# Seven products instead of eight in the first layer of three experts, running sums in PSUM, and all sums on VectorE

## The chip, the core and the metric

The kernel runs on one core of a Trainium2 chip. The core has five engines that work through queues of their own, each in the order in which the program was laid out: TensorE (matmuls; PE in the profile, its weight loads PEld), VectorE (DVE), ScalarE (ACT), GpSimd (POOL) and SyncE (SP, which here starts DMA transfers). They wait for one another by semaphores. The metric is the time of one execution on the device in microseconds.

## The reference

Two blocks follow one another. The first is a recurrent attention (RWKV-5) over 4 batches, 8 heads, 768 steps and a head size of 48; its output becomes `x`, 3072 rows of 384. The second gives each row to one of eight experts, 384 rows to each, and sends it through that expert's two layers:

```python
def _moe_ref(x, w_gate, w1, w2):
    N, D = x.shape                       # 3072, 384
    E = w_gate.shape[1]                  # 8
    cap = N // E                         # 384
    order = np.argsort(-(x @ w_gate).flatten())
    ...                                  # the best pairs (row, expert) first, until an expert is full
    for e in range(E):
        mask = assigned == e
        h = np.maximum(x[mask] @ w1[e], 0.0)    # 384x384 times 384x1024
        out[mask] = h @ w2[e]                   # 384x1024 times 1024x384
```

All inputs and the output are fp32.

## The kernel before

**Attention (0 to about 150 us)** runs in `Mild` over units of 128 steps of one batch. The change does not touch it.

**The search.** `Assignment` finds which expert fills next and with which rows, without leaving the chip. One round of `likely_steps` compares every row's value with 16 candidates (`ind`, L932), counts with matmuls (`counts`, L944 and L955, the second of which reads `wide`) and narrows the interval three times, mostly on VectorE; then come `acc`, a matmul for the places (`st_ps`, L1075), `row`, `oh` and `vals`, and two small matmuls (`some_ps` L1408, `list_ps` L1426) that give the list of rows `tok`. So VectorE and TensorE hand this chain to and fro while TensorE works on an expert.

**The experts.** `Experts.run` goes through the experts in the order in which they fill, n = 1 to 8; n = 8 is the rest of an expert that was begun during the attention and has 128 rows. While expert n is worked on, `later` takes the search on, and `fetch` gathers the rows of the next expert (`xg`, on POOL's queue) and loads its weights (`load_weights`, on SP's queue, w2 first, then w1). Weights and rows lie in two sets of buffers, `turns[n % 2]`, so expert n+2 is loaded when expert n releases its own.

For each expert of 384 rows:

- `turn` transposes the gathered rows to `xT`: three blocks of 128 inner elements, 384 rows wide.
- `hidden` is the first layer: for each of eight tiles of 128 of the 1024 hidden columns, three matmuls (one for each inner block) of a 128x128 weight tile with 384 columns of `xT`, summed in one bank of PSUM; ScalarE writes the ReLU to `hid`.
- The second layer of experts 1 to 5 is `seven` for the first 256 rows. `hid` and w2 are cut in halves both ways, and the four products of halves are had from seven, with sums of blocks before and after (Winograd's form of Strassen's scheme). `sums_of` makes the sums of blocks on VectorE: T1 to T4 of w2 (768 elements a lane), S1 to S4 of `hid` (512). `products` runs the matmuls in groups, one bank a group; ScalarE copies each group to `res`, and VectorE adds there (`SEVEN_OUT`, eight sums of 192 elements). The last 128 rows go through `result`, eight matmuls of 384 columns.
- The second layer of experts 6 and 7 (`many`) is `fifteen`, by fifteen products for all 384 rows, with eleven sums of `hid` (two of them, `EARLY_SUMS`, made at half of the first layer), ten of w2 and 24 of the results.

Order: the framework's scheduler lays out each engine's queue from the program order and its own estimates; nothing in this part is placed by hand, apart from `issue_after` for the first expert. An instruction that waits holds up everything behind it on its engine.

Names in what follows: `hid<-h_ps` is the ReLU (L1543), `h_ps` the first layer (L1541), `p_ps` the products (L1616), `o_ps` the last 128 rows (L1643), `S`, `T`, `H` and `W` the sums of blocks (L1593).

Of the kernel before, what the change touches and what calls it, by code (L numbers as in the profile page):

```python
# [10 lines left out]
F32 = mybir.dt.float32  # L11
# [4 lines left out]
AF = mybir.ActivationFunctionType  # L16
# [1432 lines left out]
def rwkv5_eagle_then_base_layer_balanced(  # L1449
# [12 lines left out]
    nc = tc.nc  # L1462
# [21 lines left out]
    class Experts:  # L1484
# [7 lines left out]
        def open_rest(self, ctx, **how):  # L1492
            pool = lambda name, bufs, **kw: ctx.enter_context(tc.tile_pool(name=name, bufs=bufs, **kw))
            self.h, self.o, self.sums = pool("f_h", 2, **how), pool("f_o", 2, **how), pool("f_sums", 1, **how)
            self.ps_t, self.ps_h, self.ps_o = (pool(f"f_ps_{x}", 2, space=PSUM, **how) for x in "tho")

        def load_weights(self, n, fmax):
# [34 lines left out]
        def turn(self, ahead):  # L1532
            *_, xT = self.turned(ahead, lambda c: self.ps_t.tile([128, KD, 128], F32, name="xT_ps"))
            return xT

        def hidden(self, w1, xT, m, half, progress):
            hid = self.h.tile([128, KF, CAP], F32, name="hid")
            for j in range(KF):
                h_ps = self.ps_h.tile([128, CAP], F32, name="h_ps")
                for f in range(KD):  # L1540
                    nc.tensor.matmul(h_ps[:, 0:m], w1[:, f, ts(j, 128)], xT[:, f, 0:m],  # L1541
                                     start=(f == 0), stop=(f == KD - 1))
                nc.scalar.activation(hid[:, j, 0:m], h_ps[:, 0:m], AF.Relu)  # L1543
                if j == KF // 2 - 1:
                    half(hid)
                progress((j + 1) / KF)
            return hid
# [1 line left out]
        BLOCKS = dict(h0=(0, 0), h1=(0, 1), h2=(1, 0), h3=(1, 1), h4=(2, 0), h5=(2, 1))  # L1549
        SEVEN_EARLY = (("S3", "h0", SUB, "h2"),)  # L1550
        SEVEN_LATE = (("S1", "h2", ADD, "h3"), ("S2", "S1", SUB, "h0"), ("S4", "h1", SUB, "S2"))
        SEVEN = ((("p1", "h0", "w0"), ("p2", "h1", "w2")), (("p7", "S3", "T3"), ("p5", "S1", "T1")),
                 (("p6", "S2", "T2"), ("p3", "S4", "w3")), (("p4", "h3", "T4"),))
        SEVEN_OUT = ((("o0", "p1", ADD, "p2"),), (), (("u2", "p1", ADD, "p6"), ("u3", "u2", ADD, "p7"),
                     ("u4", "u2", ADD, "p5"), ("o1", "u4", ADD, "p3"), ("o3", "u3", ADD, "p5")),
                     (("o2", "u3", SUB, "p4"),))
        EARLY_SUMS = (("H1", "h0", ADD, "h2"), ("H11", "h0", SUB, "h4"))
        HID_SUMS = (("H8", "h1", ADD, "h3"), ("H7", "h1", SUB, "h0"), ("H9", "h1", SUB, "H11"),
                    ("H3", "h5", SUB, "H9"), ("H0", "h1", ADD, "h2"), ("H6", "h3", ADD, "h5"),
                    ("H5", "H11", ADD, "H6"), ("H2", "h2", SUB, "H6"), ("H12", "H2", ADD, "h4"))  # L1560
        W2_SUMS = (("W11", "w0", "w3"), ("W7", "w0", "w1"), ("W9", "W7", "w3"), ("W13", "W9", "w4"),
                   ("W0", "W13", "w5"), ("W14", "W0", "w2"), ("W12", "w0", "w2"), ("W5", "W12", "w3"),
                   ("W6", "W5", "w5"), ("W2", "W6", "w4"))
        PRODUCTS = ((("p4", "h4", "w1"), ("p1", "H1", "w2"), ("p11", "H11", "W11"), ("p10", "h5", "w4")),
                    (("p8", "H8", "w5"), ("p13", "h1", "W13"), ("p7", "H7", "W7"), ("p9", "H9", "W9")),
                    (("p3", "H3", "w3"), ("p0", "H0", "W0"), ("p14", "h2", "W14"), ("p5", "H5", "W5")),
                    (("p12", "H12", "W12"), ("p6", "H6", "W6"), ("p2", "H2", "W2")))
        OUT_SUMS = ((),
                    (("x", "p9", SUB, "p4"), ("u", "x", SUB, "p7"), ("o0", "u", ADD, "p11"), ("t", "p13", SUB, "p11"),
                     ("o1", "t", SUB, "x"), ("o7", "p10", ADD, "p4")),  # L1570
                    (("o6", "u", ADD, "p3"), ("y", "p13", ADD, "p14"), ("z", "y", SUB, "p0"), ("o2", "p1", SUB, "z"),
                     ("o5", "z", ADD, "p8"), ("d", "p11", SUB, "p5"), ("v", "p1", ADD, "d")),
                    (("g", "p12", SUB, "o6"), ("o3", "g", SUB, "v"), ("q", "p6", SUB, "o5"), ("o8", "q", ADD, "v"),
                     ("a", "p14", SUB, "p2"), ("b", "p10", ADD, "p6"), ("o4", "a", SUB, "b")))
# [7 lines left out]
        def seven_w2(self, w2):  # L1582
            H, D = KF // 2, DX // 2
            at = {f"w{2 * j + k}": w2[:, ts(j, H), ts(k, D)] for j in range(2) for k in range(2)}
            self.sums_of(at, (("T3", "w3", SUB, "w1"), ("T1", "w1", SUB, "w0"), ("T2", "w3", SUB, "T1"),
                              ("T4", "T2", SUB, "w2")), D)
            return at

        def sums_of(self, at, which, n=128):
# [7 lines left out]
        def fifteen(self, left, right, tok, rows, at_product):  # L1597
            self.products(self.PRODUCTS, self.OUT_SUMS, left, right, tok, rows, at_product, KD, NC)

        def seven(self, left, right, tok, rows, at_product):  # L1600
            self.products(self.SEVEN, self.SEVEN_OUT, left, right, tok, rows, at_product, 2, 2)

        def products(self, products, out_sums, left, right, tok, rows, at_product, nk, ni):
            D = DX // nk
# [35 lines left out]
        def result(self, c, hid, w2, tok, to):  # L1640
# [8 lines left out]
            nc.scalar.copy(o_sb, o_ps)  # L1649
            self.scatter(o_sb, tok[:, c:c + 1], to)  # L1650

        def run(self, ahead, later, rows, pulls={}, xT=None):
            xT, lead = xT or self.turn(ahead), True
            while ahead:
                n, _, tok, w1, w2 = ahead
                nb = tok.shape[1]
                whole = nb == NC
                many = whole and n in (E - 2, E - 1)
                ahead = next((a for a in later if a), None)
                late, lead = lead and not many, False  # L1660
                right = (self.fifteen_w2 if many else self.seven_w2)(w2) if whole and not late else None
                left = {}
                some = pulls.get(n, 2)
                due = [1.55, 1.75] if some == 2 else [0.75 + 1.15 * i / (some - 1) for i in range(some)]

                def half(hid):
                    nonlocal right
                    for name, (i, j) in self.BLOCKS.items():
                        left[name] = hid[:, ts(j, KF // 2), ts(i, 128)]
                    last = self.sums_of(left, self.EARLY_SUMS if many else self.SEVEN_EARLY)  # L1670
                    if late:
                        with tc.issue_after(last.ins):
                            right = self.seven_w2(w2)

                def progress(t):
                    nonlocal xT
                    while due and t > due[0]:
                        due.pop(0)
                        next(later, None)
                        if many and not due and ahead:  # L1680
                            xT = self.turn(ahead)

                def at_product(part):
                    progress(1 + part)

                hid = self.hidden(w1, xT, nb * 128, half if whole else lambda hid: None, progress)
                if whole:
                    self.sums_of(left, self.HID_SUMS if many else self.SEVEN_LATE)
                    (self.fifteen if many else self.seven)(left, right, tok, rows, at_product)
                    if many:  # L1690
                        continue
                for c in range(NC - 1 if whole else 0, nb):
                    if c == nb - 1 and ahead:
                        xT = self.turn(ahead)
                    self.result(c, hid, w2, tok, next(rows))

        def early(self, ps, pool, w1, w2, xg, tok, rows, have):
# [182 lines left out]
```

## Time and profile before

| | |
|---|---|
| Median of 3 runs | 398.09 us (398.03 to 398.3) |
| The profiled execution | 397.39 us |
| its span, from the first to the last instruction | 395.7 us |
| granted TensorE clock, mean | 0.997 |
| first layer, TensorE: 384 instructions | 120.7 us busy |
| products of the second layers, 128x192 `p_ps<-w,hid`: 80 instructions | 14.7 us busy, 333 ns one |
| the last 128 rows of five experts and the eighth: 96 instructions | 33.1 us busy |
| ScalarE's ReLU, 128x384: 56 instructions | 27.5 us busy, 491 ns one |
| weight transfers: 18 of 1.5 MB | 10.2 us median from issue to landing |

A page lists for each engine how long it was busy, for forty equal slices of the span in tenths how busy each engine was, then the costliest groups of instructions by line. A group's row has the shape, the count, the busy time, the mean length of one, the engine's idle time just before, and what ended that. A length of a matmul runs to its modelled end, beyond the start of the next one, so the spacing of starts says more than the length. The stages of the experts are found in TensorE's timeline: expert 2 runs from 188.0 to 220.5 us, expert 3 to 253.1, expert 4 to 285.7, expert 5 to 317.7, expert 6 to 348.3, expert 7 to 378.1 and the rest to the end.

### The profile page before, as it was taken

The page shows a single profiled execution, that of the slowest core. Times are in us where ns is not written, and L with a number is a line of the kernel's source. Part 1 is how long each engine was busy: PE and PEld are TensorE (multiplying, and loading weights), DVE is VectorE, ACT ScalarE, POOL GpSimd, SP SyncE. Part 2 cuts the span into 40 slices and gives each one's busy share as a digit, 9 for nine tenths or more (in the row PEclk, how much of TensorE's full clock was granted, in tenths as well). Part 3 has the DMA queues.
Part 4 walks back from the last instruction along what each step waited for, and adds up shares of the span by engine and source line. Part 5 has one row for each costly group of instructions (what it writes and reads, how often), then busy time and mean ns, then how long its engine had stood idle before and what let it go on. Part 6 is the DMA issues. An engine that isn't in the chain of part 4 may idle for free. (4 is left out here: it accounts for less than half of the span.)

```text
span 395.7 us, 8692 instructions
## 1 busy us (share of the span) xinstructions
PE 381.1 (96%) x3243; PEld 289.3 (73%) x3243; DVE 266.9 (67%) x934; ACT 162.0 (41%) x429; POOL 138.4 (35%) x173
## 2 busy tenths in 40 slices
PE   7899999999999999999999999999999999999993
PEld 5678888888877765587578569558757856966991
DVE  6755777576885677897839819979578663952630
ACT  4998888888873312222222122121222222222130
POOL 7888877666732013032121120302303211040020
PEclk9999999999999999999999999999999999999998
DMA  9999999898692155371460650109209173380010
GB/s 120 156 183 200 200 173 205 156 169 157 117 342 81 42 200 217 96 282 42 160 239 16 214 210 2 60 0 333 87 21 354 59 275 131 92 308 2 2 61 27
DMA packets 95331, 57.29 MB, mean 145 GB/s; under 512 B 77232, under 2 KB 89520, under 8 KB 95280
## 3 DMA queue, kind: packets, MB, share of 16 engines
q1 hardware_dynamic: 91936, 47.21, 47.7%
q0 software_dynamic: 3104, 9.44, 6.8%
q8 instruction: 27, 0.44, 0.5%
q14 instruction: 24, 0.20, 0.2%
q10 hardware_dynamic: 240, 0.00, 0.0%
HBM read 47.20 MB, written 9.44 MB: 143 GB/s over the span
## 5 line engine op out<-in xcount | busy, mean ns | idle before, releaser
L1541 PE MATMUL h_ps<-xT,w 128*128 128x384 f32 (+1 forms) x384 | 120.7, 467 | 0.6 <-ACT xT L1529 0.6
L1541 PEld LDWEIGHTS h_ps<-xT,w 128*128 128x128 f32 x384 | 66.4, 190 | 38.1 <-issue 2.5
L1543 ACT ACTIVATE hid<-h_ps 128x384 f32<-128x384 f32 (+1 forms) x64 | 29.7, 465 | 91.1 <-PE h_ps L1541 85.1
L495 ACT ACTIVATE AT<-ident,dd 128x128 f32<-128x128 f32 x192 | 59.6, 391 | 1.9 <-DVE dd L448 1.8
L1513 POOL DMA_INDIRECT xg<-x_rows,tok x22 | 22.4, 1017 | 95.6 <-PE h_ps L1541 32.1
L1637 POOL DMA_INDIRECT out_dram<-o_all,to x16 | 17.9, 1120 | 94.6 <-DVE o_all L1625 62.2
L508 DVE COPY_PREDICATED AT<-mask,g_ps 128x512 f32<-128x512 uint8 x48 | 32.6, 733 | 12.1 <-PE g_ps L504 10.6
L1620 ACT COPY res<-p_ps 128x384 f32<-128x384 f32 (+2 forms) x28 | 13.3, 474 | 60.5 <-PE p_ps L1616 60.5
L1643 PE MATMUL o_ps<-w,hid 128*128 128x384 f32 x96 | 33.1, 488 | 0.0
L504 PE MATMUL g_ps<-rT,kT 48*128 48x128 f32 x384 | 27.9, 284 | 0.7 <-DVE AT L508 0.6
L436 POOL TENSOR_TENSOR kss<-krs,wk 128x384 f32<-128x384 f32 x24 | 24.3, 1015 | 8.0 <-DVE krs L340 5.5
L504 PEld LDWEIGHTS g_ps<-rT,kT 48*128 48x128 f32 x384 | 23.4, 187 | 4.0 <-PE unread_ps L418 0.5
L542 PE MATMUL y_ps<-AT,vts 128*64 128x128 f32 x384 | 25.7, 276 | 0.0
L443 POOL TENSOR_TENSOR rk<-rk,u_bc 128x384 f32<-128x384 f32 x24 | 24.2, 1007 | 1.9
L442 POOL TENSOR_TENSOR rk<-krs 128x384 f32<-128x384 f32 x24 | 24.5, 1020 | 0.2 <-DMA krs<-in_r_dram 0.2
L1643 PEld LDWEIGHTS o_ps<-w,hid 128*128 128x128 f32 x96 | 17.2, 190 | 9.5 <-issue 0.2
L542 PEld LDWEIGHTS y_ps<-AT,vts 128*64 128x64 f32 x384 | 20.6, 137 | 1.2 <-issue 0.7
L1616 PE MATMUL p_ps<-T,S 128*128 128x192 f32 x120 | 20.9, 328 | 0.0
L1593 DVE TENSOR_TENSOR H<-hid 128x512 f32<-128x512 f32 x12 | 7.9, 686 | 19.1 <-ACT hid L1543 19.1
L1616 PEld LDWEIGHTS p_ps<-T,S 128*128 128x128 f32 x120 | 19.6, 190 | 0.1
L932 DVE TENSOR_TENSOR own<-counts,same 128x64 f32<-128x64 f32 x21 | 4.7, 222 | 21.7 <-PE counts L944 21.6
L1616 PE MATMUL p_ps<-w,hid 128*128 128x192 f32 (+1 forms) x112 | 19.0, 316 | 0.0
(303 smaller groups left out, 694.0 us busy)
## 6 DMA issues: line engine op xcount, KB each, us to landing
w<-in_moe_w_dram SPq DMA_DIRECT2D x18, 1536.0 KB, 10.2
krs<-in_k_dram SPq DMA_DIRECT2D x24, 192.0 KB, 4.0
krs<-in_r_dram SPq DMA_DIRECT2D x24, 192.0 KB, 4.7
vts<-in_v_dram SPq DMA_DIRECT2D x24, 192.0 KB, 4.7
x_rows<-xr SPq DMA_DIRECT2D x24, 192.0 KB, 3.2
xg<-x_rows,tok POOLq DMA_INDIRECT x22, 4.4
out_dram<-o_all,to POOLq DMA_INDIRECT x16, 2.8
out_dram<-o_sb,to POOLq DMA_INDIRECT x5, 3.0
```

Source lines behind the costliest of these rows:

```text
L436: self.nc.gpsimd.tensor_mul(self.kss[:, n % self.NS].rearrange("p (g h) d -> p g h d", g=2)[:, :, :, 0:D], src, self.wk.rearrange("p (g h) ...
L442: nc.gpsimd.tensor_mul(rk, self.krs[:, n % self.NK, 1, 0:H, 0:D], self.krs[:, n % self.NK, 0, 0:H, 0:D])
L443: nc.gpsimd.tensor_mul(rk, rk, self.u_bc)
L495: nc.scalar.mul(AT[:, z, a, :], self.ident, dd[:, h:h + 1])
L504: nc.tensor.matmul(g_ps[:, z, a, :], kT[rows, a, :], rT[rows, a, :], start=True, stop=True)
L508: nc.vector.copy_predicated(out=AT[:, z], mask=self.mask.unsqueeze(1).to_broadcast([128, HP, T]), data=g_ps[:, z])
L542: nc.tensor.matmul(yv[q * PD:(q + 1) * PD, o // 2, o % 2, :], lhsT, rhs, start=(o // 2, q) not in seen, stop=stop, skip_group_check=True)
L1513: nc.gpsimd.indirect_dma_start(out=xg[:, c, :], out_offset=None, in_=x_dram[0:within, :], in_offset=bass.IndirectOffsetOnAxis(ap=tok[:, c: ...
L1541: nc.tensor.matmul(h_ps[:, 0:m], w1[:, f, ts(j, 128)], xT[:, f, 0:m], start=(f == 0), stop=(f == KD - 1))
L1543: nc.scalar.activation(hid[:, j, 0:m], h_ps[:, 0:m], AF.Relu)
L1616: nc.tensor.matmul(ps[:, q, :], left[a][:, j, :], right[b][:, j, :], start=(j == 0), stop=(j == KF // 2 - 1))
L1643: nc.tensor.matmul(o_ps, hid[:, j, ts(c, 128)], w2[:, j, :], start=(j == 0), stop=(j == KF - 1))
```

## The change

1. **First layer of experts 3, 6 and 7** (`FIRST_BY_SEVEN`): `hidden_by_seven` takes the place of `hidden`. The rows are cut in two halves of 192, the 1024 hidden columns in two halves of 512; of the three inner blocks the first two are taken by the seven products, the third is added plainly inside the same banks. `FIRST` lists the pairs of operands of each product. The four column tiles of a half are done two at a time (p = 0, 1). Each product goes on in the PSUM bank of an earlier one, so that partial sums add up there: P6, P7 and P4 in the bank of P1, P3 in that of P5. ScalarE copies P1, P5 and P6 out, VectorE adds a later bank to a copy in place, ScalarE does the ReLU.
2. Its sums of weights and rows are new: `weight_sums`, four of 512 elements a lane, is called in the second layer of the expert ahead, and `row_sums`, five of 192, right after its rows are turned. A new pool `f_first` holds them.
3. **Second layer, `seven`**: also with running sums in PSUM, in the order P1, P2, P5, P6, P3, P7, P4. Four products are copied out, three sums on VectorE and one copy on ScalarE give the output. T4 has its sign turned, so that P4 adds. The rows ahead are turned before P4 instead of before the last 128 rows.
4. **`fifteen`**: all eleven sums of `hid` come after the first layer, in a new order, and the products and output sums are ordered so that those without sums come first.

```diff
+        def weight_sums(self, w1):
+            H = F // 2
...
+            for name, a, op, b in (("T1", "b1", SUB, "b0"), ("T2", "b3", SUB, "T1"), ("T3", "b3", SUB, "b1"),
+                                   ("T4", "b2", SUB, "T2")):
+                t = self.first.tile([128, H], F32, name=f"first_{name}")
+                nc.vector.tensor_tensor(out=t, in0=at[a], in1=at[b], op=op)
...
+        def row_sums(self, xT):
+            H = CAP // 2
...
+            for name, a, op, b in (("S1", "a2", ADD, "a3"), ("S2", "S1", SUB, "a0"), ("S4", "a1", SUB, "S2"),
+                                   ("S5", "d0", SUB, "d1"), ("S3", "a0", SUB, "a2")):
...
+        FIRST = {"P1": (("a0", "b0"),), "P2": (("a1", "b2"), ("d0", "c0")), "P5": (("d1", "c1"), ("S1", "T1")),
+                 "P6": (("S2", "T2"),), "P7": (("S3", "T3"),), "P3": (("S5", "c1"), ("S4", "b3")),
+                 "P4": (("d1", "c0"), ("a3", "T4"))}
+        FIRST_ORDER = ("P1", 0), ("P2", 0), ("P5", 0), ("P6", 0), ("P1", 1), ("P7", 0), ("P3", 0), ("P4", 0), \
+            ("P5", 1), ("P6", 1), ("P2", 1), ("P7", 1), ("P3", 1), ("P4", 1)
+
+        def hidden_by_seven(self, x, w, progress):
...
+            def keep(p, name, ps):
+                t = self.sums.tile([128, Q, H], F32, name=f"kept_{name}", tag=f"sum_False_{5 + 3 * p + len(kept) % 3}")
+                nc.scalar.copy(t, ps)
...
+            def block(p, i, f, src):
+                nc.scalar.activation(hid[:, ds(f * KF // 2 + p * Q, Q), ts(i, H)], src, AF.Relu)
+
+            def added(p, i, f, name, other):
+                t = kept[name, p]
+                nc.vector.tensor_tensor(out=t, in0=t, in1=other, op=ADD)
+                block(p, i, f, t)
+
+            for step, (name, p) in enumerate(self.FIRST_ORDER):
+                ps, fresh = bank(p, {"P2": "C", "P5": "B", "P3": "B"}.get(name, "A"))
+                pairs = self.FIRST[name]
+                for a, b in pairs:
+                    for q in range(Q):
+                        nc.tensor.matmul(ps[:, q, :], w[b][:, ts(p * Q + q, 128)], x[a], start=fresh,
+                                         stop=(a, b) == pairs[-1], skip_group_check=True)
+                        fresh = False
+                if name in ("P1", "P5", "P6"):
+                    keep(p, name, ps)
+                elif name == "P2":
+                    added(p, 0, 0, "P1", ps)
+                elif name == "P7":
+                    added(p, 1, 1, "P5", ps)
+                elif name == "P3":
+                    added(p, 0, 1, "P6", ps)
+                else:
+                    block(p, 1, 0, ps)
...
-        SEVEN = ((("p1", "h0", "w0"), ("p2", "h1", "w2")), (("p7", "S3", "T3"), ("p5", "S1", "T1")),
-                 (("p6", "S2", "T2"), ("p3", "S4", "w3")), (("p4", "h3", "T4"),))
...
+        SEVEN = (("P1", "h0", "w0"), ("P2", "h1", "w2"), ("P5", "S1", "T1"), ("P6", "S2", "T2"), ("P3", "S4", "w3"),
+                 ("P7", "S3", "T3"), ("P4", "h3", "T4"))
...
+        def seven(self, left, right, tok, rows, at_product, between):
...
+            for step, (name, a, b) in enumerate(self.SEVEN):
...
+                if name == "P4":
+                    between()
...
+        FIRST_BY_SEVEN = 3, 6, 7
...
+                def turn():
+                    nonlocal xT, row_sums
+                    if ahead:
+                        xT = self.turn(ahead)
+                        if after:
+                            row_sums = self.row_sums(xT)
...
+                    if after and t > 1.1 and not weight_sums:
+                        weight_sums = self.weight_sums(ahead[3])
```

## The prediction

> **What bounds the kernel now.** I read the totals and the forty slices of the page first, then TensorE's timeline, then VectorE's busy time by stage. The chain of waits goes back only to 381 us, so the bound is read from TensorE itself.
>
> ```profile
> PE 381.1 (96%) x3243; PEld 289.3 (73%) x3243; DVE 266.9 (67%) x934; ACT 162.0 (41%) x429; POOL 138.4 (35%) x173
> ...
> PE   7899999999999999999999999999999999999993
> ...
> PEclk9999999999999999999999999999999999999998
> ```
>
> TensorE works in every slice from the second to the last but one, at full clock. The page says that a busy PE need not be at its peak, so the test is the spacing of its instructions (start, length, count):
>
> ```profile
> 226.05 10.57 PE L1541 MATMUL h_ps<-xT,w 128*128 128x384 f32 x32
> 236.45 0.25 PE L944 MATMUL counts<-prop,ind 128*128 128x64 bf16 x3
> ...
> 302.43 2.76 PE L1616 MATMUL p_ps<-w,hid 128*128 128x192 f32 x16
> 305.03 4.06 PE L1616 MATMUL p_ps<-T,S 128*128 128x192 f32 x24
> 308.93 1.46 PE L1616 MATMUL p_ps<-w,S 128*128 128x192 f32 x8
> ```
>
> From start to start, 32 of 384 columns take 10.40 us (0.325 each) and 40 of 192 columns take 6.50 us (0.1625 each). The trace counts an fp32 matmul twice: a full expert's first layer is 24 matmuls in the code and 48 here. TensorE therefore sets the end from 155 us on, a matmul removed is time removed, and a wait on TensorE is time added.
>
> **What is removed.** For experts 3, 6 and 7 the first layer is 48 instructions of 384 columns, 15.6 us. By seven products it is eleven pairs of operands (the rows of FIRST) times four column tiles = 44 matmuls, 88 instructions of 192 columns, 14.3 us. That saves 1.3 us for each expert, **3.9 us** in all. The second layer keeps its 28 matmuls per expert and fifteen products keep their 60, so reordering saves nothing there.
>
> A rule speaks against this. The Trainium skill, "TensorE: Matmul & The Clock Gate", section "Back-to-back issue gap", gives a stream of weight loads and matmuls about 81 ns at 128 columns and 131 at 512: nearly a fixed price per matmul. A line through those two makes 192 columns cost 0.78 of 384, by which the first layer would take 88 x 0.325 x 0.78 = 22.3 us, and the three experts would lose 20 us. The rows above are this kernel's own fp32 stream with a weight load before each matmul, and halve exactly. I take the rows.
>
> **What is added, and beside what.**
>
> ```profile
> L477 DVE TENSOR_TENSOR rT<-rT_ps,WR 112x512 f32<-112x512 f32 x23 | 15.8, 685 | 4.6 <-PE rT_ps L458 4.6
> ...
> L1593 DVE TENSOR_TENSOR S<-hid 128x512 f32<-128x512 f32 x10 | 6.8, 680 | 2.2 <-ACT hid L1543 2.2
> ...
> L1625 DVE TENSOR_TENSOR o_all<-res 128x192 f32<-128x192 f32 x20 | 6.4, 351 | 0.0
> L1620 ACT COPY res<-p_ps 128x384 f32<-128x384 f32 x17 | 8.2, 480 | 38.1 <-PE p_ps L1616 38.1
> ```
>
> Per chosen expert VectorE gets four weight sums (512 wide, 0.68; two in a row at 307.36 us take 1.28, so 0.60 apart), 2.4 us; five row sums (0.35, some 0.27 apart), 1.4 us; and six additions of 384 elements with one operand in PSUM. No row has that addition. It lies between 0.35 (192 wide) and 0.685 (112x512 from PSUM); by width I take 0.55. ScalarE gets six copies of 0.48, 2.9 us; it is busy 7.5 us of 32 in such a stage, and the cost is zero but for their place in the chain. In each of five seven-product second layers, three sums on VectorE replace eight: 1.25 us less there. ScalarE makes five copies of 192 for four (0.3 us, hidden).
>
> The price is order, since every engine runs its queue in order. VectorE's busy time by stretch (columns: stretch, its length, busy PE, PEld, DVE, ACT, POOL with counts, clock, DMA share, GB/s):
>
> ```profile
> 203.50:204.00 0.50, 0.50 (x3) 0.23 (x3) 0.00 (x0) 0.00 (x0) 0.00 (x0) 1.00 0.65 255
> 204.00:204.50 0.50, 0.50 (x6) 0.27 (x5) 0.00 (x0) 0.00 (x0) 0.00 (x0) 1.00 0.05 18
> ...
> 204.30:220.50 16.20, 16.20 (x95) 13.42 (x94) 15.07 (x58) 3.59 (x8) 1.99 (x2) 1.00 0.07 26
> 302.40:317.70 15.30, 15.30 (x83) 12.99 (x82) 10.33 (x20) 3.59 (x8) 5.18 (x5) 1.00 0.40 154
> 333.70:348.30 14.60, 14.60 (x132) 14.44 (x131) 13.43 (x31) 3.50 (x7) 1.42 (x1) 1.00 0.36 119
> ```
>
> - **Expert 2's second layer** (204.3 to 220.5). VectorE is busy 15.07 of 16.2 us. Weight and row sums for expert 3 add 3.8, the shorter output sums take 1.25: 17.6, or 1.4 over. By the queue: the first weight sum stands ahead of expert 2's S1 and waits for w1 of expert 3, whose transfer ends at 204.0 (255 GB/s before, 18 after). Behind it are S1, S2, S4, the search's count, an output sum and `wide`: three weight sums, S1, T4, S2 and S4 at 0.60 and 0.9 us of small ones end at 209.1. TensorE reaches the matmul that reads `wide` after P1, P2, P5 and one matmul of P6, at 204.4 + 13 x 0.325 = 208.6, and waits with the semaphore: **0.4**. S1 itself is ready at 206.5, before P5 at 207.1. Later five row sums and T4 (2.3 us) stand in the search's chain; `acc` moves from 219.3 to 221.0, and the matmul that took it at 220.48 waits **0.3**. Two hairline waits for `ind` and the next `wide`: **0.2**.
> - **Expert 3's first layer.** `vals` follows `acc` by 4.2 us (in the trace 5.7, of which 2.0 of the next search's preparation now come later; 0.5 is the new addition); the twelve matmuls before the token list take 3.9. The list and the one after it wait **0.4**. A reader starts 0.2 us after the matmul's slot ends (`most` at 285.93, the slot of its `counts` over at 285.73). P4 needs P7 added; P3 (1.3 us) lies between, against 0.2 + 0.55: covered. P7 needs ScalarE's copy of P6, with P1 of the other half (0.65) between and 0.2 + 0.48 needed: a hairline, and whatever ScalarE is late comes on top.
> - **Expert 5's second layer.** 10.33 + 2.55 = 12.9 of 15.3, fits. S1 now feeds the third product instead of the fourth; it is done at 304.8, P5 starts at 305.03. Nothing.
> - **Expert 6.** w1 of expert 7 lands at about 329.2 (the transfer's 417 GB/s fall to 255 over 328 to 330) and its first weight sum stands ahead of two of expert 6's additions; T1, both additions: P7 is added by 331.1, just when TensorE reaches P4. With the token list, **0.15**. Its fifteen products start with operands that need no sum, then use each sum 0.89 us apart while VectorE makes them 0.60 apart.
> - **Expert 7.** VectorE has 13.43 of 14.6 in expert 6's products; two sums moved there (1.2) and five row sums (1.4) make 16.0. The excess goes into expert 7's first layer ahead of its first addition, which comes at 351.0; the copy of P6 is queued behind that addition's ReLU on ScalarE, so P7 is **0.35** late, and the list **0.2**, where before already waited 0.36: net **0.2**.
> - **Experts 1 and 4**: `wide` behind one more output sum, **0.1**.
>
> No DMA is added. The order of weight loads, gathers and scatters on SP's and POOL's queues is unchanged; scatters of the two row blocks still wait for P4, as o2 did.
>
> Sum: -3.9 + 0.4 + 0.3 + 0.2 + 0.4 + 0.15 + 0.2 + 0.1 = -2.1. Against the profiled execution (span 395.7, its time 397.39) that is 393.6 and 395.3. The median of the runs shown is 0.7 higher, 398.09, and the forecast on it is **396.0**.
>
> **Rivals.** A difference under 0.2% (0.8 us) cannot be told from no change here.
> - *Clean*, 20%: every new wait falls into slack, 398.1 - 3.9 = 394.2, up to 395.0. For it: the busy stretches overlap little with what TensorE needs at once. Against it: 17.6 us of work in a 16.2 us stretch.
> - *Eaten*, 15%: the waits are twice what I counted (3.5 us), 397.7. For it: I followed one queue at a time, and a wait on TensorE can delay VectorE's next. Against: a late TensorE also gives VectorE time.
> - *Slower*, 10%: VectorE's queue stuck on w1 of expert 3. Each us that the transfer ends after 204.0 delays `wide`, from 204.6 on P5 too, and TensorE by one. With the 1.75 us of waits already counted, an end at 207.0 makes it 0.8 slower, 398.9; later, more. For: the load is issued only when expert 1's w2 is released, and shares the engines with a gather. Against: the trace has it at 204.0, and neither release nor gather moves.
> - That fewer matmuls do not come out is excluded by the code: 88 x 192 columns against 48 x 384.
>
> The forecast itself, 395.0 to 397.0, has 55%. The range, 394.2 to 397.7, takes in the clean end and twice the waits; outside lie the slower case and part of the eaten one. Faster gets the clean case, the forecast and a little of the third, 0.77; same 0.14; slower 0.09.
>
> **What would show it.** First-layer matmuls of experts 3, 6, 7 at 192 columns and 0.1625 us spacing; VectorE waiting for `w` once near 204 us before `first_T`; TensorE late at `counts<-wide`, `st_ps` and `some_ps` between 208 and 227 us, and at P7's matmul some 4 us into expert 7. Expert 6 to 7 should be 1.2 us nearer, expert 2 to 4 hardly. A spacing above 0.17, or waits inside the second layers of experts 1, 4 and 5, would make it wrong.

## The result and the profile after

| | before | after |
|---|---|---|
| Median of 20 runs each | 398.26 us (397.84 to 399.22) | 396.91 us (396.29 to 399.42) |
| The profiled execution, its span | 397.39, 395.7 us | 396.99, 395.2 us |

The ratio of after to before is **0.9971 (95% interval 0.9962 to 0.998)**: faster by 1.15 us (0.8 to 1.5). The forecast was 396.0 in a range of 394.2 to 397.7, so the time is inside it and the gain about half of what was forecast. The single profiled executions differ by 0.4 us only (0.5 in their spans), since before's was quicker than any of its 20 runs; so what is read from them stage by stage need not add up to the medians. Single executions of after lie further apart than those of before, which will matter below.

The totals and two rows of the forty slices of the page of after:

```profile
PE 381.2 (96%) x3363; PEld 307.0 (78%) x3363; DVE 281.6 (71%) x959; ACT 169.1 (43%) x452; POOL 141.1 (36%) x173
...
PE   8999999999999999999999999999999999999993
...
PEclk9999999999999999999999999999999999999998
```

TensorE is still the bound, at the same clock (0.996 granted, 0.997 before). It has 120 instructions more and is busy for the same time, so busy time says nothing here; the spacing does. TensorE's timeline in expert 3's first layer of after (start, length, count):

```profile
228.88 0.81 PE L1597 MATMUL h_ps<-xT,first_T 128*128 128x192 f32 x4
229.53 0.81 PE L1597 MATMUL hb_ps<-xT,w 128*128 128x192 f32 x4
230.18 0.81 PE L1597 MATMUL hb_ps<-first_S,first_T 128*128 128x192 f32 x4
230.83 0.81 PE L1597 MATMUL h_ps<-first_S,first_T 128*128 128x192 f32 x4
```

Four of 192 columns every 0.65 us, 0.1625 each, as the forecast had it. VectorE's rows of after by form (busy, mean ns, idle before):

```profile
L1544 DVE TENSOR_TENSOR first_T<-w 128x512 f32<-128x512 f32 x6 | 4.0, 688 | 8.1 <-DMA w<-in_moe_w_dram 8.1
...
L1589 DVE TENSOR_TENSOR kept_P<-kept_P,hc_ps 128x384 f32<-128x384 f32 x6 | 3.3, 548 | 8.1 <-PE hc_ps L1597 4.1 <-ACT kept_P L1581 4.0
L1555 DVE TENSOR_TENSOR first_S<-xT 128x192 f32<-128x192 f32 x9 | 2.9, 353 | 0.1
```

The addition of 384 elements with an operand in PSUM costs 0.55 us, the value taken. Weight sums cost 0.69, row sums 0.35. The 8.1 us in front of `first_T` are two waits for w1, in experts 2 and 6.

Where the time went is seen by expert. From the first `h_ps` of one expert to that of the next, in TensorE's timeline (us; the other columns are kernels described below; expert 8 is its first layer alone):

| expert | before | after | second_only | first_only | hybrid_behind |
|---|---|---|---|---|---|
| 1 | 32.92 | 33.17 | 33.16 | 32.94 | 32.93 |
| 2 | 32.52 | 32.75 | 32.74 | 32.48 | 32.66 |
| 3 (first layer by seven) | 32.56 | 31.49 | 33.00 | 31.90 | 31.79 |
| 4 | 32.64 | 33.22 | 33.10 | 32.64 | 32.64 |
| 5 | 32.00 | 32.45 | 32.14 | 32.00 | 32.00 |
| 6 (by seven) | 30.67 | 29.58 | 30.85 | 30.52 | 29.58 |
| 7 (by seven) | 29.71 | 29.16 | 30.19 | 29.39 | 29.34 |
| 8 | 5.36 | 5.85 | 5.85 | 5.84 | 5.83 |

In after, experts 3, 6 and 7 give 1.07, 1.09 and 0.55: 2.71 us. Experts 1, 2, 4 and 5 take back 0.25, 0.23, 0.58 and 0.45, and expert 8 another 0.49. Together that is -0.71; the attention before them ended 0.21 later in this execution, which leaves the 0.5 us of the spans. The losses stand mostly where no first layer is changed. Counted from `h_ps` to the first product, the first layers of experts 3, 6 and 7 themselves got 1.03, 1.09 and 0.54 us shorter, 2.66 of the 3.9 us.

VectorE's busy time in the second layers of experts 2, 5 and 6 of after (stretch, length, busy PE, PEld, DVE, ACT, POOL, clock, DMA share, GB/s):

```profile
204.70:221.20 16.50, 16.50 (x96) 13.44 (x95) 15.84 (x55) 3.46 (x10) 2.00 (x2) 1.00 0.08 26
302.60:318.40 15.80, 15.75 (x85) 13.02 (x83) 12.87 (x25) 3.37 (x9) 4.84 (x5) 1.00 0.39 150
333.25:348.00 14.75, 14.75 (x138) 14.59 (x136) 14.37 (x33) 3.83 (x8) 0.88 (x1) 1.00 0.30 98
```

VectorE is fuller, as forecast, though less so where it was nearly full: 15.84 of 16.5 us in expert 2 (17.6 us of work forecast), 14.37 of 14.75 in expert 6 (16.0 forecast), 12.87 in expert 5 (12.9 forecast). Of expert 2, the timeline of VectorE in after (start, length):

```profile
203.94 1.29 DVE L1544 TENSOR_TENSOR first_T<-w 128x512 f32<-128x512 f32 x2 [4.74 <-DMA w<-in_moe_w_dram]
205.15 0.68 DVE L1544 TENSOR_TENSOR first_T<-w,first_T 128x512 f32<-128x512 f32 x1
205.75 0.69 DVE L1666 TENSOR_TENSOR S<-hid 128x512 f32<-128x512 f32 x1
...
208.75 0.28 DVE L932 TENSOR_TENSOR wide<-digit_of,cnt 128x128 f16<-128x128 f32 x1
```

This is the queue that the prediction followed by hand: the first weight sum stands ahead of S1 and waits for w1 until 203.94, and `wide` is ready at 209.03 where 209.1 was forecast. But TensorE loses nothing there: expert 2 began 0.46 us later than before while w1 landed at the same time, so TensorE came to `counts<-wide` behind one matmul of P6 at 209.16, not at 208.6. Time lost earlier covered the wait.

### The profile page after: what moved, and what is told of

It is laid out like the page before. It is cut to its first block, busy times and chain, and to the rows that moved or that the text cites. A ratio compares the mean times of both kernels' runs of the same rounds, so it can differ in the third digit from the quotient of the medians.

```text
span 395.2 us, 9027 instructions
## 1 busy us (share of the span) xinstructions
PE 381.2 (96%) x3363; PEld 307.0 (78%) x3363; DVE 281.6 (71%) x959; ACT 169.1 (43%) x452; POOL 141.1 (36%) x173
## 4 chain that ended last, share of the span: by engine, by line
PE 66%; issue 10%; DVE 9%; ACT 4%; POOL 4%; DMA 4%; POOLq 0%; another core or an unknown queue 0%; SPq 0%; DVEq 0%
PE h_ps L1618 12%; PE o_ps L1749 7%; PE y_ps L542 6%; PE pa_ps L1691 6%; PE g_ps L504 4%; PE h_ps L1597 4%; PE hb_ps L1597 3%; PE e_h_ps L1840 3%; PE e_o_ps L1848 3%; PE pb_ps L1691 3%; ACT AT L495 2%; PE kT_ps L458 2%; PE kv_ps L521 2%; PE x_ps L591 2%; DMA w<-in_moe_w_dram 2%
## 5 line engine op out<-in xcount | busy, mean ns | idle before, releaser
L1618 PE MATMUL h_ps<-xT,w 128*128 128x384 f32 (+1 forms) x240 | 72.7, 453 | 0.8 <-ACT xT L1530 0.6
L1618 PEld LDWEIGHTS h_ps<-xT,w 128*128 128x128 f32 x240 | 39.7, 191 | 21.3 <-issue 2.2
L1743 POOL DMA_INDIRECT out_dram<-o_all,to x16 | 20.8, 1300 | 84.4 <-DVE o_all L1731 22.2
L1620 ACT ACTIVATE hid<-h_ps 128x384 f32<-128x384 f32 (+1 forms) x40 | 17.8, 447 | 55.2 <-PE h_ps L1618 50.6
L1749 PE MATMUL o_ps<-w,hid 128*128 128x384 f32 x96 | 32.5, 490 | 0.0
L560 ACT COPY x<-y_ps 128x512 f32<-128x512 f32 x24 | 14.0, 584 | 12.2 <-PE y_ps L542 12.2
L477 DVE TENSOR_TENSOR rT<-rT_ps,WR 112x512 f32<-112x512 f32 x23 | 15.7, 685 | 4.6 <-PE rT_ps L458 4.6
L448 DVE TENSOR_REDUCE dd<-rk 128x8 f32<-128x384 f32 x24 | 13.1, 546 | 6.6 <-POOL rk L443 6.6
L458 PE MATMUL rT_ps<-ident,krs 128*112 128x128 f32 x96 | 15.3, 281 | 0.5 <-DMA krs<-in_r_dram 0.3
L1722 PE MATMUL p_ps<-W,H 128*128 128x128 f32 x128 | 15.8, 275 | 0.0
L1691 PE MATMUL pa_ps<-T,S 128*128 128x192 f32 x80 | 15.8, 331 | 0.0
```

Of the source, the lines that this page charges most:

```text
L458: self.nc.tensor.transpose(ps[0:PD + self.D, a, :], self.pair(t, a), self.ident)
L1691: nc.tensor.matmul(ps, left[a][:, j, :], right[b][:, j, :], start=(j == 0 and name in ("P1", "P2", "P5")), stop=(j == KF // 2 - 1), skip_g ...
L1749: nc.tensor.matmul(o_ps, hid[:, j, ts(c, 128)], w2[:, j, :], start=(j == 0), stop=(j == KF - 1))
```

## Experiments

Two questions: are the losses those of the weight and row sums, as predicted, or of the second layers written anew? And does the order of VectorE's queue decide, or the amount of its work? Comparisons are with before on the same chip.

| kernel | median us | ratio to before (95%) |
|---|---|---|
| second_only | 400.24 (399.93 to 400.76) | 1.0057 (1.0044 to 1.007) |
| first_only | 397.28 (396.07 to 401.38) | 0.999 (0.9973 to 1.0007) |
| turn_back | 397.32 (396.91 to 398.94) | 0.9986 (0.9974 to 0.9997) |
| w1_late | 397.18 (396.77 to 398.84) | 0.9986 (0.9975 to 0.9997) |
| first_only_w1 | 396.9 (396.35 to 400.36) | 0.9974 (0.995 to 0.9997) |
| hybrid | 396.38 (395.47 to 398.5) | 0.9961 (0.995 to 0.9972) |
| hybrid_all | 401.01 (400.42 to 402.21) | 1.0075 (1.0055 to 1.0095) |
| act_pad | 397.57 (396.37 to 399.5) | 0.9987 (0.9964 to 1.0011) |
| after_behind | 396.87 (396.53 to 397.2) | 0.9972 (0.996 to 0.9983) |
| after_again | 396.61 (396.2 to 398.25) | 0.9973 (0.9963 to 0.9983) |
| **hybrid_behind** | **395.97 (395.77 to 396.17)** | **0.9948 (0.9935 to 0.9961)** |
| tail_between | 397.12 (396.5 to 397.74) | 0.9987 (0.9979 to 0.9995) |

### The two halves of the change

second_only:

```
-        FIRST_BY_SEVEN = 3, 6, 7
+        FIRST_BY_SEVEN = ()
```

> No expert's first layer by seven products; only the second layers are the new ones (running sums in PSUM, next expert's transposes ahead of P4, P5 as the third product). Theory A, that the new second layers themselves lose time: of the trace of after, the distance from first layer to first layer is 0.25 us longer in expert 1, 0.58 in expert 4 and 0.45 in expert 5, where no first layer by seven is at work; so this run is 1.0 to 1.3 us slower than before (ratio 1.0025 to 1.0033) and xg is again waited for some 0.4 us near 279. Theory B, that the losses come from the added weight and row sums on VectorE: within 0.3 us of before.

Slower by 2.3 us by the ratio, more than either theory had it. Theory B falls: with no weight or row sum at work, experts 1, 2 and 4 lose 0.24, 0.22 and 0.46, much as in after, expert 5 a third (0.14), and experts 3, 6 and 7, whose first layers are plain here, another 0.44, 0.18 and 0.48. On top of this kernel the first layers by seven bring 3.4 us (0.9971 against 1.0057), near the 3.9 counted. But not all of the 2.3 us is lost in after too. Expert 3's 0.44 is a wait of the search's matmul for VectorE, in its first layer:

```profile
224.58 0.31 PE L1408 MATMUL some_ps<-vals,row 128*128 128x48 f16 x6 [0.30 <-DVE vals L932]
```

Expert 7 waits in the same way 0.67 us for `list_ps`, 0.36 before. And the new order of the fifteen products costs 0.18 and 0.17 us behind the plain first layers of experts 6 and 7.

first_only has the second layers of before (`seven`, `fifteen`, `HID_SUMS`, the transposes' place) and the new first layers. One sum is written in place:

```
-("u4", "u2", ADD, "p5"), ("o1", "u4", ADD, "p3")
+("o1", "u2", ADD, "p5"), ("o1", "o1", ADD, "p3")
```

> First layers of experts 3, 6 and 7 by seven products, second layers as before (products copied out by ScalarE and summed from SBUF on VectorE; one sum is written in place to save space, which costs nothing). Theory A: three first layers bring 3.9 us less some 1.4 of waits, 2.4 to 2.8 us faster than before, 395.5 to 395.9 on the median of 398.26, faster than after by 1.3. Theory B: VectorE has more sums still than in after, so its waits grow and it is no faster than after, 0 to 1.2 us faster than before.

Half right. Experts 1, 2, 4 and 5 lost nothing (the table above). But expert 6 gained 0.15 and expert 7 0.32 instead of 1.1 and 0.5: the time was that of before within the interval (0.9 us less by the medians). The halves do not add up, and the stages show one reason. From the first product to the next expert, experts 6 and 7 take 14.71 and 13.73 us in before, and 14.71 and 13.72 in after; the old order of the fifteen products behind a first layer by seven (first_only) takes 15.07 and 14.04, the new order behind a plain one (second_only) 14.89 and 13.90. Each order suits its own first layer: new first layers with the old order lose 0.7 us here, the new order with plain first layers 0.35, and both changed together nothing.

### Where a second layer with running sums loses

TensorE's timeline at the end of expert 1's products, before:

```profile
181.77 0.83 PE L1528 MATMUL xT_ps<-ident,xg 128*128 128x128 f32 x6
182.43 0.81 PE L1643 MATMUL o_ps<-w,hid 128*128 128x384 f32 x2
183.08 0.49 PE L1528 MATMUL xT_ps<-ident,xg 128*128 128x128 f32 x3
```

and after:

```profile
180.64 0.82 PE L1529 MATMUL xT_ps<-ident,xg 128*128 128x128 f32 x6
181.29 0.51 PE L1691 MATMUL pa_ps<-T,hid 128*128 128x192 f32 x2
181.75 0.55 PE L1529 MATMUL xT_ps<-ident,xg 128*128 128x128 f32 x3
182.14 1.14 PE L1691 MATMUL pa_ps<-T,hid 128*128 128x192 f32 x6
```

The transposes of the third block of rows need the bank of the first, which ScalarE must have copied. Before, two matmuls of 384 columns (0.65 us) stood between, and the starts follow without a gap. Now it is two of 192 columns: 0.325 us of work from 181.29 to 181.75, a gap of 0.14, and 0.06 more after the transposes. That is most of expert 1's 0.25. (At the same place in expert 4 of after_behind the profile names the copy: 0.31 us of waiting for ScalarE's `xT`.) In expert 4 the earlier place has a second price:

```profile
277.77 0.91 PE L1529 MATMUL xT_ps<-ident,xg 128*128 128x128 f32 x6
278.51 0.49 PE L1691 MATMUL pa_ps<-T,hid 128*128 128x192 f32 x2
279.38 0.52 PE L1529 MATMUL xT_ps<-ident,xg 128*128 128x128 f32 x3 [0.38 <-DMA xg<-x_rows,tok]
```

The third block of rows is just arriving. It was read at 280.83 before. With 0.18 us of `some_ps` waiting for `vals` at 269.5, that is about expert 4's 0.58. turn_back moves the transposes (and row sums) back behind P4:

```
-                    self.seven(left, right, tok, rows, at_product, turn)
+                    self.seven(left, right, tok, rows, at_product, lambda: None)
...
-                    if c == nb - 1 and not whole:
+                    if c == nb - 1:
```

> As after, but the transposes of the next expert's rows (and the row sums) come behind P4, ahead of the last 128 rows, as in before. Theory A: the wait for xg in expert 4 (0.38 us) and the hairline waits for the third transposes go, 0.4 to 0.7 us faster than after (396.2 to 396.5). Theory B, that the transposes' place is of no weight because TensorE only waits elsewhere: within 0.2 us of after; slower than after by 0.3 or more if the row sums of experts 3 and 6, now later by P4's 1.3 us, come too late for the first layer.

The wait for xg went and expert 4 took 32.87, 0.35 less; expert 1 took 33.22, expert 2 33.12 and expert 3 31.76, 0.05, 0.37 and 0.27 more; the median is 0.4 us above after's where theory A had 0.4 to 0.7 below. What took the wait's place, in the weight loads of turn_back in expert 1:

```profile
181.20 1.27 PEld L1691 LDWEIGHTS pa_ps<-T,hid 128*128 128x128 f32 x8 [0.25 <-ACT kept_P L1696]
```

(In experts 2, 3 and 5 it is 0.31, 0.27 and 0.26.) P7 and P4 add into the same bank, and ScalarE must have copied it after P7 before P4 adds to it. With separate products in `res` there was no such order between two products; a running sum in PSUM makes one, and needs something to stand between P7 and P4. The transposes did that in after. tail_between puts the last 128 rows there (built on after_behind, below):

```
+                def between():
+                    self.result(NC - 1, hid, w2, tok, next(rows))
+                    turn()
...
-                    self.seven(left, right, tok, rows, at_product, turn)
-                for c in range(NC - 1 if whole else 0, nb):
+                    self.seven(left, right, tok, rows, at_product, between)
+                for c in range(NC if whole else 0, nb):
```

> As after_behind, but in the five second layers by seven products the eight matmuls for the last 128 rows, and then the next expert's transposes, come between P7 and P4, instead of the transposes alone between them and the last rows at the end. Theory A (the running sum is what costs: P4 adds into the bank that ScalarE must first have copied P7 out of, so something must stand between; the transposes are a poor filler, since the third waits for ScalarE's copy of the first and their rows are just arriving): with 2.6 us of matmuls there, P4 waits for nothing, the rows are there, and experts 1, 2, 4 and 5 take 32.95, 32.5, 32.7 and 32.0 us as before the change; the time is 0.6 to 1.0 us below after_behind's 396.87, 395.9 to 396.3, the same as hybrid_behind. Theory B (the seven products lose by their sums on VectorE, not by their order on TensorE): within 0.3 us of after_behind; slower if the row sums, 1.3 us later, come late for experts 3 and 6.

A miss: ratio 0.9987, if anything worse than after_behind's 0.9972 (on another chip). Experts 1 and 4 took 33.02 and 32.73, nearly back, but expert 2 took 32.80, not 32.5; in expert 5 `o_ps` now waited 0.52 us for VectorE to read P3 out of the bank it takes (32.70 in all), and expert 3 took 32.29, 0.4 of its 0.5 us more than in after_behind in the second layer, in gaps of 0.05 to 0.18 that no single wait explains. So the filler helps where the transposes had lost most, and brings its own bank with it; by the time alone theory B is not ruled out. The plainest measure of the running sums comes below, from after_behind and hybrid_behind.

### Order or amount on VectorE

w1_late:

```
-                    if after and t > 1.1 and not weight_sums:
+                    if after and t > 1.6 and not weight_sums:
```

> As after, but the four weight sums for experts 3, 6 and 7 are put on VectorE after the fifth product of the expert before (tenth of fifteen) instead of after the first. Theory A (VectorE held up by w1 of expert 3): the first weight sum no longer waits at 204, wide of the search is ready near 207 instead of 209.1, expert 3 starts 0.2 to 0.4 us earlier after expert 2, and the sum is 0.2 to 0.4 us faster than after. Theory B (the amount of VectorE's work decides, not its order): the four sums then stand in the chain before acc, which stays at 221 or comes later, and the time is the same or slower by up to 0.5 us; in experts 6 to 7 weight sums come into the first layer and cost P5 or P6 a wait.

Inconclusive by its edit: the scheduler laid the weight sums out early all the same, and the first still waited 4.45 us, to 204.24. Only `wide` moved ahead of S4, to 207.8; expert 2 took 32.73, as in after. first_only_w1 tried the same place for expert 7 alone:

```
+                    if after and t > (1.6 if many else 1.1) and not weight_sums:
```

> First layers by seven, second layers as before (as first_only), but the weight sums for expert 7 are put on VectorE after the tenth of expert 6's fifteen products instead of after the second. In first_only expert 6 took 30.52 us (before 30.67), VectorE stood 4.1 us at first_T until w1 of expert 7 was there at 329.8, two additions stood behind it, and TensorE waited 0.31 for kept and 0.27 for hid. Theory A (that queue place is what ate expert 6's gain): expert 6 takes 29.8 us, 0.6 to 0.8 less, time 0.6 to 0.8 us less than first_only's 397.28. Theory B (ScalarE or the old order of the fifteen products is what was late): expert 6 stays within 0.2 us of 30.52.

Here too `first_T` stayed ahead of expert 6's additions (329.91) and expert 6 took 30.57. Place in the program is not place in the queue. hybrid gives first_only_w1 the new order of the fifteen products:

> As first_only_w1, with the new order of the fifteen products (operands without sums first); so first layers by seven and fifteen products as in after, seven products as in before, weight sums for expert 7 late. Stage by stage from the traces of before (experts 1, 2, 4, 5), first_only (3) and after (6, 7): 1.8 us less than before, 2.3 if expert 8's first layer had not grown by 0.5; 1.1 less than after. Theory A (seven products in running sums is what costs after its gain): 396.0 to 396.5 against 398.26 of before. Theory B (VectorE with eight sums per second layer is too full): expert 3 loses, and the time is that of after or more.

396.38, in the band of theory A, though by the medians only 0.5 below after, and the executions spread over 3 us. Expert 6 took 29.58 and expert 7 29.17. In this execution w1 of expert 7 landed at 328.94, 0.97 us earlier than in first_only_w1, while expert 6 began at 317.49 in both. The two causes stand in different places: 0.36 of the 0.99 us between them is in the fifteen products, the order; 0.63 is in the first layer, where the fifteen products have no part. There TensorE waits in first_only_w1 for an addition that stands behind `first_T`, and does not in hybrid (first_only_w1, then hybrid):

```profile
331.59 0.92 PE L1597 MATMUL h_ps<-xT,w 128*128 128x192 f32 x4 [0.36 <-DVE kept_P L1589]
```

```profile
331.06 0.81 PE L1597 MATMUL h_ps<-xT,w 128*128 128x192 f32 x4
```

In after w1 landed as long after expert 6's start as in hybrid (11.4 us, against 12.4), and expert 6 took the same 29.58. So one us later costs TensorE 0.6. To take this away the weight sums were bound behind VectorE's own work, with the call that the kernel has for its first expert (`self.held` is the last of S1, S2, S4, or the last addition of a first layer by seven). after_behind is after with this edit:

```
-                        weight_sums = self.weight_sums(ahead[3])
+                        with tc.issue_after(self.held.ins):
+                            weight_sums = self.weight_sums(ahead[3])
```

> As after, but the weight sums are bound behind VectorE's own work of the expert at hand: for expert 3 and 6 behind the last of S1, S2, S4 of the expert before, for expert 7 behind the last addition of expert 6's first layer. The DMA of w1 and all work are the same, only the queue place changes. Theory A (VectorE held up at w1 costs time, more in executions where the transfer ends late, which is why after's times reach from 396.3 to 399.4 where those of before and of second_only stay within 1.5 us): the times come together, none above 398 but one in ten, and the median is 0.3 to 0.8 us lower, 396.1 to 396.6; expert 2's second layer is not shorter than 16.3. Theory B (the spread has another source): spread and median as after, or worse where the sums come too late for the first layer.

> The changed kernel itself, on the same chip as the two variants and as before, so that they can be compared: 396.9, spread 396.3 to 399.4 as in its first runs.

VectorE in after, while expert 6's first layer ends:

```profile
329.81 0.69 DVE L1544 TENSOR_TENSOR first_T<-w 128x512 f32<-128x512 f32 x1 [3.32 <-DMA w<-in_moe_w_dram]
330.42 0.55 DVE L1589 TENSOR_TENSOR kept_P<-kept_P,hc_ps 128x384 f32<-128x384 f32 x1
330.92 0.56 DVE L1589 TENSOR_TENSOR kept_P<-kept_P,h_ps 128x384 f32<-128x384 f32 x1
```

and in hybrid_behind, which binds the sums in the same way:

```profile
329.33 0.55 DVE L1589 TENSOR_TENSOR kept_P<-kept_P,hc_ps 128x384 f32<-128x384 f32 x1 [3.64 <-PE hc_ps L1597]
329.98 0.55 DVE L1589 TENSOR_TENSOR kept_P<-kept_P,h_ps 128x384 f32<-128x384 f32 x1
331.21 0.55 DVE L1589 TENSOR_TENSOR kept_P<-kept_P,hb_ps 128x384 f32<-128x384 f32 x1 [0.68 <-PE hb_ps L1597]
331.69 1.28 DVE L1544 TENSOR_TENSOR first_T<-w 128x512 f32<-128x512 f32 x2
```

The additions now wait for TensorE alone, and the weights have long landed when they are read. In after_behind's expert 2, `wide` was ready at 206.5, 2.5 us sooner, and expert 2 still took 32.69 (32.75). Sums made later also cost something: experts 3 and 7 took 31.77 and 29.34 us, in after 31.49 and 29.16 (hybrid_behind loses so in experts 2 and 7, 32.66 and 29.34 against hybrid's 32.48 and 29.17). So the median stayed (0.9972 against 0.9973 on one chip), and theory A is right on the spread alone: six executions within 0.7 us, none above 397.2, where after reached 398.25 on the same chip and 399.42 in its first 20. Six are few, but the two other kernels that bind the sums, hybrid_behind and tail_between, agree: of all 25 executions none is more than 1.3 us above the fastest of its kernel, against 36 of 116 of the kernels that make weight sums unbound. That VectorE's place in line makes the time depend on when a transfer ends is what these runs support; no slow execution was profiled, so the late transfer itself was not seen in one.

hybrid_behind is hybrid with the same edit:

> As hybrid (seven products as before the change, fifteen and first layers as in after), with the weight sums bound behind VectorE's own work as in after_behind. Theory A: 0.3 to 0.8 us below hybrid's 396.38, 395.6 to 396.1, with the upper times (397 to 398.5) gone. Theory B: as hybrid.

**395.97, ratio 0.9948 (0.9935 to 0.9961)**, 2.1 us faster than before and below the interval of after on the same chip (0.9963 to 0.9983). Its range is 0.4 us. It differs from after_behind in the second layers by seven products alone (products, their sums, the transposes' place), on the same chip, and no execution of one reaches the other's: the running sums cost 0.9 us (395.97 against 396.87), by stage 0.24 in expert 1, 0.46 in expert 4 and 0.13 in expert 5, nothing elsewhere beyond 0.04. It beats both kernels: the seven products of before, fifteen products and first layers of after, weight sums behind the work at hand.

### All experts

```
-        FIRST_BY_SEVEN = 3, 6, 7
+        FIRST_BY_SEVEN = 2, 3, 4, 5, 6, 7
```

> As hybrid, with the first layers of experts 2, 4 and 5 by seven products as well. Theory A (a first layer by seven brings about 1.0 us wherever it is used): 2 to 3 us faster than hybrid. Theory B (VectorE has no room: 15.07 us busy of 16.2 in expert 2's second layer before the change, and 2.4 us of weight and 1.4 of row sums are added in each): the search's chain comes late, TensorE waits for st_ps, some_ps and list_ps, and the time is within 1 us of hybrid, or slower.

Theory B, and 4.6 us slower than hybrid, worse than it had it. TensorE's timeline in expert 4 of hybrid_all:

```profile
278.53 2.10 PE L1719 MATMUL o_ps<-w,hid 128*128 128x384 f32 x6
283.04 1.03 PE L1529 MATMUL xT_ps<-ident,xg 128*128 128x128 f32 x6 [2.41 <-DMA xg<-x_rows,tok]
```

Experts 2 and 3 still gain (31.84 and 31.77 us). In expert 4 VectorE is busy 15.10 us of the 17 from 253, in hybrid 13.88; `list_ps` comes at 276.62 instead of 271.46, the gather follows it to 278.15 from 273.45, and TensorE stands 2.41 us for its rows, and 1.25 in expert 5. Work on VectorE costs when it stands in the search's chain, whose end is a gather.

### Expert 8

act_pad (its time is from few runs, and not told from after's):

```
+            pad = self.sums.tile([128, 1], F32, name="pad")
+            for _ in range(3):
+                nc.scalar.copy(pad, left["h0"][:, 0, 0:1])
```

> As after, with three copies of one column (results unused) ahead of each of the two sets of fifteen products, six more ScalarE instructions. In the traces of all five kernels with the new code the sixth ReLU of expert 8 comes 0.5 us late while its product is long there (idle 0.9 instead of 0.4) and TensorE loses 0.5; in before none does. Theory A (bound to the place in ScalarE's stream of instructions): with six more ahead of it the late one is another ReLU, or none. Theory B (bound to what else runs at that time, such as the scatter of the last rows): it stays the sixth. The copies themselves cost nothing, as ScalarE is busy under half the time there.

ScalarE's timeline in after (act_pad has the same wait at the same instruction):

```profile
380.00 0.28 ACT L1620 ACTIVATE hid<-h_ps 128x128 f32<-128x128 f32 x1 [0.39 <-PE h_ps L1618]
380.67 0.28 ACT L1620 ACTIVATE hid<-h_ps 128x128 f32<-128x128 f32 x1 [0.39 <-PE h_ps L1618]
381.87 0.45 ACT L1620 ACTIVATE hid<-h_ps 128x128 f32<-128x128 f32 x2 [0.92 <-PE h_ps L1618]
```

ReLUs come every 0.67 us; the sixth comes 1.2 us after the fifth, with its product long done, and TensorE runs out of banks. Six more ScalarE instructions did not move it, so theory A falls as it was put. It stays the sixth in every kernel with the new code but tail_between, whose expert 8 took 5.36 us as before. The cause is open.

## Why the prediction was right, and where it was not

- **Bound and spacing: right.** 0.1625 us at 192 columns. Of the two prices weighed, the row held; the gap in the Trainium skill ("TensorE: Matmul & The Clock Gate", "Back-to-back issue gap"), from whose figures the prediction estimated a loss of 20 us, does not describe this fp32 stream. The count of 3.9 us gross held too (88 instructions in place of 48, at these spacings); 2.66 us of it arrived in the three first layers.
- **The sum of the waits: too small, and in the wrong places.** 1.75 us was counted; the profiled executions lose 3.2 us from expert 1 to 8, and the interval's 1.15 us leaves 2.75, nearer to the rival *Eaten* (3.5) than to the count. The time fell into the range because that reached to twice the waits, and because most of expert 2's 0.9, half of the count, did not come while others did. That much was luck.
- **Costs on VectorE: right in size.** 0.55, 0.69 and 0.35 us; its busy time grew by 14.7 us over the span, and the prediction's own costs add up to 15. The 1.25 us saved per second layer holds (11.4 us of output sums before, 5.2 after, in five), though the count behind it does not: before makes seven output sums there, 35 in the trace, and not eight (and 20, not 24, behind fifteen products).
- **Expert 2 (0.9 forecast): 0.23, and not by that cause.** `wide` (0.4): no wait. `st_ps` behind `acc` (0.3): `acc` ended at 221.06 as forecast, the matmul lost 0.17. But second_only has no weight sums and loses the same 0.22, and after_behind, with `wide` 2.5 us earlier, the same 0.17. Nor is it the running sums alone, for hybrid_behind has none and loses 0.14. What takes it is open.
- **Expert 3 (0.4): about 0.25** (1.07 of 1.3 us arrived). **Expert 6 (0.15): 0.2.** **Expert 7 (net 0.2): 0.75.** `list_ps` lost 0.76 in place of the 0.36 of before, and some 0.3 went in gaps of 0.05 to 0.1 in the first layer, which I had not counted. P7, the part that was followed by hand, came with a gap of 0.05.
- **Experts 1 and 4 (0.1), expert 5 ("Nothing"): 0.25, 0.58 and 0.45. This is the step that failed:** "The second layer keeps its 28 matmuls per expert and fifteen products keep their 60, so reordering saves nothing there". I took that to mean that it costs nothing; I credited it with 1.25 us of VectorE per expert and did not ask what a running sum adds to TensorE's order. It adds the copy between P7 and P4 (0.25 us where nothing stands between them), and its filler puts the transposes before shorter cover (0.2 in expert 1) and before their rows (0.38 in expert 4). With the weight sums bound the running sums cost 0.9 us, after_behind against hybrid_behind. For the fifteen products the sentence fails the other way: beside a first layer by seven their new order saved 0.7 us. The prediction said in one clause what would make it wrong ("waits inside the second layers of experts 1, 4 and 5"), and that is what came.
- **Expert 5 in particular.** P5 as the third product: S1 was ready at 305.38, 0.6 later than the 304.8 forecast, since VectorE's `W` waited for w2 of expert 6 to 303.36. In second_only, w1_late and after_again the expert took 32.14 to 32.18, so 0.3 of the 0.45 belongs to that one execution.
- **Expert 8 (not forecast): 0.49**, cause open.
- **The slower rival** had a mechanism that expert 6 shows at work (0.6 us of TensorE for w1 1 us later), and the wrong place for this execution: w1 of expert 3 ended at 203.94, as in before. Five of after's 20 times lie above 397.5 where before's stay within 1.4 us, and with the sums bound no execution came more than 1.3 us above its kernel's fastest; which of the two transfers was late in the five is not known.

## What to carry to other kernels

A sum kept in PSUM trades additions for an order: each product that adds to a bank waits for whoever must first copy that bank, so look for what will stand in between, and whether that has cover of its own. Count the parts of a change that "keep the same work" too; here the running sums took back 0.9 of 2.1 us. Try the parts of a change one at a time, but do not add up what they gave: the order of the fifteen products lost time beside either first layer that it was not made for. And an instruction that reads a transfer belongs behind the queue's other work unless someone needs it sooner, which has to be bound, since a later place in the program does not give it.

## What was not expected of the hardware

- In this stream of fp32 matmuls, each with its own weight load, TensorE's time per instruction follows the columns down to 192 (0.1625 us, half of the 0.325 at 384): halving the columns and nearly doubling the number costs nothing.
- A VectorE addition of 384 fp32 elements with one operand in PSUM took 0.55 us, on the line from 0.35 at 192 to 0.69 at 512, both from SBUF; at 192 with one operand in PSUM it took 0.35 too. The operand in PSUM cost nothing that these rows show.
- The late sixth ReLU of expert 8 (0.5 us), in eleven of the twelve profiled kernels with new code, at the same instruction; its cause is open.
